# A recurrent attention and MoE kernel: stage 0 turned before its decay, diagonals moved off TensorE in four stages, and a shorter look-ahead in the pair loop

## The chip, the cores and the metric

The kernel runs on one core of a Trainium2 chip. The metric is the device time of one execution in microseconds (us); lower is better. Engines: TensorE (PE, with its weight loads as PEld), VectorE (DVE), ScalarE (ACT), GpSimd (POOL), SyncE (SP), and 16 DMA engines.

## The reference

Per batch (4) and head (8) a 48 x 48 state decays along 768 steps; each output row is read from the state plus a diagonal term with its own weight u. The result goes through a two-layer network with a leaky ReLU.

```
for t in range(768):
    cur = einsum(u * k[t], v[t]);  y[t] = einsum(r[t], state + cur)
    state = w[:, None] * state + einsum(k[t], v[t])
x = y as (3072, 384);  h = x @ w_in (384 x 2048);  out = max(0.01*h, h) @ w_out (2048 x 384)
```

## The kernel before, in words

**Tiling.** A stage is 128 time steps of one batch, all 8 heads: 24 stages, numbered chunk by chunk (stage n is chunk n // 4 of batch n % 4). Within a stage the decay is put into the operands: q = r * w^(t-64) and k' = k * w^(63-t), by two tables `qtab` and `ktab` made once with exp of an exponent times ln w. q and k' are turned (transposed) to `tp`; their product A, cut by a strict triangle `mask`, is the attention inside the stage; the state `st` brings in the earlier chunks.

**The letters.** A list ORDER, written out in the source, gives the program order of the whole start: the tables, the attention of the first stages (0 to 9, and some of 10 and 11) and the network of stages 0 to 5 in part. Each engine plays its own items of it in that order, and semaphores are derived from what is read and written. A letter and a stage: k, r, v loads (POOL queue; those of stage 0 for k on ACT and r on SP); wi, wo weight loads (POOL); P the DVE product with a table (L344; q or k half); T the turn by four TensorE matmuls with the identity (L398) and t its eviction on ACT (L412) or DVE (L410, "@"); X the DVE product q*k' (L359), or with a final T the turn by a DMA transpose issued by SP (L349) instead of T and t; A the eight matmuls of q with k' (L423); M the two masked evictions (L432, L436); D four matmuls of width 2 that give the diagonal sums (L451); Q the scaling of v by them on DVE (L366); Y the matmuls that form y (three with `vs` and the identity, L550, and 16 to 28 of 32 columns, L557) and y their eviction to xT on ACT (L571); K the four matmuls of k' with v (L464) and S the state on DVE (L522, or L525 and L527); G a group of 12 matmuls of the first layer for one stage (L596) and g its leaky eviction (L606); J and j the same for a pair of stages (L619, L629); H and h the second layer of a stage (16 matmuls, L643) with its eviction (L655) and store (SP, L657); F a number of filling matmuls on ones (L260).

**Two kinds of diagonal.** In a stage below DIAG the diagonal goes D, Q and the three matmuls with `vs`. In a later stage DVE makes row sums of r*k*u (L373, L375, L377, letter q), POOL makes two tiles `at` with them on the diagonal (L384, letter Q there), and the masked eviction writes over the rest with a predicate (L436).

**Two kinds of turn.** Stages below TURNED are turned on TensorE, the others by the DMA transpose.

**Start.** w is spread to all partitions by two fp32 matmuls (L295), ACT takes its ln (L301) and makes the tables (L306), DVE applies them to stage 0 (L344), and only then TensorE turns stage 0. w's columns (L484, L485) feed the decay table of the state. POOL makes `ident` and `mask` (L266, L270).

**Pair loop.** After ORDER a loop over pairs m = 3 to 11 of stages (2m, 2m+1) plays eight J of the pair; row sums and diagonal tiles of stages 2m+4, 2m+5; loads of 2m+8, 2m+9; P and DMA turn of 2m+6, 2m+7; H of 2m-2; A of 2m+4, 2m+5; Y and y of 2m+2, 2m+3; M, K and S of 2m+4, 2m+5; H of 2m-1. Banks of PSUM (8) are handed out in program order, first freed first taken.

Of the kernel before, what the change touches and what calls it, by code (L numbers as in the profile page):

```python
# [6 lines left out]
ALU = mybir.AluOpType  # L7
# [120 lines left out]
def bass_rwkv5_eagle__then__act_leaky_relu_kernel(  # L128
# [39 lines left out]
    qexp = SB("qexp", [128, 1], FP32)  # L168
# [3 lines left out]
    ones = SB("ones", [128, 256])  # L172
# [14 lines left out]
    ps = [ctx.enter_context(nc.psum_tensor(f"ps{i}", [128, 512], FP32)) for i in range(8)]  # L187
# [56 lines left out]

    def tokens():
        add("pool", lambda: G.iota(tcol[:, :], pattern=[[0, 1]], base=0, channel_multiplier=1,
                                   allow_small_or_imprecise_dtypes=True), W=["tcol"])

# [6 lines left out]
    def fill(n):  # L255
        i = free[0]

        def emit():
            for _ in range(n):
                last = PE.matmul(ps[i][:, 0:256], ones[:, 0:128], ones[:, 0:256], start=True, stop=True)  # L260
# [12 lines left out]
    def exponents():  # L273
        add("dve", lambda: V.tensor_scalar(kexp[:, :], tcol[:, :], -1.0, float(MID - 1), ALU.mult, ALU.add),
            R=["tcol"], W=["kexp"])
        add("dve", lambda: V.tensor_scalar(qexp[:, :], tcol[:, :], 1.0, float(-MID), ALU.mult, ALU.add),
            R=["tcol"], W=["qexp"])

    def zero_v():
        add("dve", lambda: V.memset(v_sb[:, :, :].rearrange("p n (h e) -> p (n h) e", e=E)[:, :, D:E], 0.0), W=["v0"])  # L280
# [9 lines left out]
    half_bank = {}  # L290

    def spread_w(half):
        ps_w, key = half_bank[half] = take()
        cols = slice(192 * half, 192 * half + 192)
        add("pe", lambda: PE.matmul(ps_w[:, cols], one_row[:, :], w_row[:, cols], start=True, stop=True),  # L295
            R=["one_row", "w_row"], W=[key])

    def log_w(half):
        ps_w, key = half_bank[half]
        cols = slice(192 * half, 192 * half + 192)  # L300
        add("act", lambda: A.activation(lnw[:, cols], ps_w[:, cols], AF.Ln), R=[key], W=[("lnw", half)])  # L301
        give(key)

    def table(dst, exps, name, half):
        cols = slice(192 * half, 192 * half + 192)
        add("act", lambda: A.activation(dst[:, cols], lnw[:, cols], AF.Exp, scale=exps[:, 0:1]),  # L306
            R=[("lnw", half), name + "exp"], W=[(name + "tab", half)])

    def small_identity():
        add("dve", lambda: V.tensor_copy(ident8[:, :], ident[0:H, 0:H]), R=["ident"], W=["ident8"])  # L310

    def wu_product():
        add("dve", lambda: V.tensor_tensor(wu_head[:, :], w_head[:, :], u_head[:, :], ALU.mult),
            R=["w_head", "u_head"], W=["wu_head"])
# [26 lines left out]
    def prep_half(n, half):  # L341
# [3 lines left out]
            R=[(name, n), ("qk"[half] + "tab", 0), ("qk"[half] + "tab", 1), ("qk0", iq)], W=[(done, iq)])  # L345
# [42 lines left out]

    turn_bank = {}

    def turn_mm(n, half):
        iq = n % NQK
        ps_t, key = turn_bank[n, half] = take()

        def emit():
            for p in range(NP):
                h0 = half * H + 2 * p
                last = PE.matmul(ps_t[:, 128 * p:128 * p + 128],  # L398
                                 qk[iq][:, h0:h0 + 2, :].rearrange("p h e -> p (h e)"), ident[:, :],
                                 start=True, stop=True)  # L400
            return last

        add("pe", emit, R=[("kp" if half else "qp", iq), ("qk0", iq), "ident"], W=[key])

    def turn_out(n, half, eng):
# [3 lines left out]
        if eng == "dve":  # L409
# [68 lines left out]
    def columns_mm():  # L478
        ps_c, key = c_bank["c"] = take()

        def emit():
            for hh in range(2):
                rows = slice(64 * hh, 64 * hh + D)
                PE.matmul(ps_c[rows, 0:H], w_head[:, :], ident8[:, :], start=True, stop=True)  # L484
                last = PE.matmul(ps_c[rows, H:2 * H], wu_head[:, :], ident8[:, :], start=True, stop=True)  # L485
            return last

        add("pe", emit, R=["w_head", "wu_head", "ident8"], W=[key])

    def every_other(ps_c, rows, c0, hh):  # L490
        return ps_c[rows, c0:c0 + H].rearrange("p (m two) -> p two m", two=2)[:, hh, :]

    def log_columns():
        ps_c, key = c_bank["c"]
        for hh in range(2):
            rows = slice(64 * hh, 64 * hh + D)
            add("act", lambda rows=rows, hh=hh: A.activation(wcol[rows, :], every_other(ps_c, rows, 0, hh), AF.Ln),
                R=[key], W=[f"wcol{hh}"])

    def decay_columns():  # L500
        ps_c, key = c_bank["c"]
        for hh in range(2):
            rows = slice(64 * hh, 64 * hh + D)
            add("dve", lambda rows=rows, hh=hh: V.tensor_copy(
                wu[rows, :, hh:hh + 1].rearrange("p m o -> p (m o)"), every_other(ps_c, rows, H, hh)),
                R=[key, f"wcol{hh}", "wu"], W=[f"wu{hh}"])
# [278 lines left out]
```

## Time and profile before

| What | Value |
|---|---|
| median of 3 runs (lowest, highest) | 170.09 us (169.96, 170.54) |
| the profiled execution's own time | 170.54 us |
| its span, first to last instruction | 168.8 us |
| busy: PE, PEld, DVE, ACT, POOL | 164.0, 124.4, 107.6, 92.5, 103.8 us |
| DMA packets moved | 19.67 MB, of which 10.03 MB on the POOL-issued queue |

How to read it: busy time is summed per engine; the chain of work that ended last names, step by step back from the end, what released the work or what stood before it on its engine. Idle time of an engine off that chain costs nothing. Durations of single instructions overlap where an engine pipelines them, so the chain's steps, and not the mean durations, are what TensorE work costs in a row. The execution's own time is 1.74 us above its span.

### The profile page before, as it was taken

What the parts mean: (1) busy time and instruction counts of PE and PEld (TensorE: products, weight loads), DVE (VectorE), ACT (ScalarE), POOL (GpSimd) and SP (SyncE); (2) the same over time, 40 slices, a digit from 0 to 9 for tenths busy, and PEclk for the clock granted to TensorE, in tenths of its full rate; (3) what the DMA queues carried; (4) which work ended last, traced back from release to release, by engine and by line L of the source; (5) the groups of instructions that cost most, each with busy time, mean ns of one, the idle gap of its engine ahead of it and who ended that gap; (6) DMA issues with size and microseconds to landing.
All of it is one profiled execution on the core that took longest, in us unless ns stands there. A gap on an engine that the chain in (4) does not pass through costs nothing.

```text
span 168.8 us, 4933 instructions
## 1 busy us (share of the span) xinstructions
PE 164.0 (97%) x2127; PEld 124.4 (74%) x2127; DVE 107.6 (64%) x215; ACT 92.5 (55%) x172; POOL 103.8 (61%) x117
## 2 busy tenths in 40 slices
PE   5999999899999999999999999999999999999994
PEld 3577899798667867867867867768768668668663
DVE  7379989884376999999859959969866050000000
ACT  3855899587123933933834835735637538449221
POOL 7999999990059979897993993993707200000000
PEclk9999999999999999999999999999999999999999
DMA  6999999999999999969999299299941011011022
GB/s 106 155 170 133 163 163 173 185 190 149 110 177 144 161 62 153 193 82 169 126 140 171 55 143 177 65 109 131 147 122 50 0 50 47 0 50 47 25 74 93
DMA packets 99146, 19.67 MB, mean 117 GB/s; under 512 B 92338, under 2 KB 99124, under 8 KB 99124
## 3 DMA queue, kind: packets, MB, share of 16 engines
q0 software_dynamic: 76512, 10.03, 93.1%
q1 hardware_dynamic: 21554, 9.12, 25.2%
q8 instruction: 17, 0.28, 0.6%
q10 hardware_dynamic: 1058, 0.20, 0.6%
q14 instruction: 5, 0.04, 0.1%
HBM read 20.45 MB, written 4.72 MB: 149 GB/s over the span
## 4 chain that ended last, share of the span: by engine, by line
PE 96%; DVE 1%; issue 1%; ACT 0%; DVEq 0%
PE ps L643 37%; PE ps L619 31%; PE ps L596 6%; PE ps L557 6%; PE ps L423 4%; PE ps L260 2%; PE ps L464 2%; PE ps L398 2%; PE ps L295 1%; PE ps L550 1%; DVE v_sb L280 1%; PE ps L451 1%; PE ps L321 0%; DVE qk L344 0%; ACT out_sb L655 0%
## 5 line engine op out<-in xcount | busy, mean ns | idle before, releaser
L643 PE MATMUL ps<-w_out_sb,gT 128*128 128x384 bf16 (+2 forms) x400 | 65.7, 320 | 0.0
L619 PE MATMUL ps<-xT,w_in_sb 128*128 128x256 bf16 x480 | 54.3, 273 | 0.0
L643 PEld LDWEIGHTS ps<-w_out_sb,gT 128*128 128x128 bf16 x400 | 37.9, 98 | 22.1
L619 PEld LDWEIGHTS ps<-xT,w_in_sb 128*128 128x128 bf16 x480 | 46.7, 98 | 6.5 <-ACT xT L571 0.2
L384 POOL TENSOR_TENSOR at<-ident,s_tok 128x512 bf16<-128x512 bf16 x32 | 35.0, 1121 | 26.8 <-DVE s_tok L377 26.8
L629 ACT ACTIVATE gT<-ps 128x512 bf16<-128x512 f32 x80 | 47.8, 597 | 6.2 <-PE ps L619 1.3
L655 ACT ACTIVATE out_sb<-ps 128x384 f32<-128x384 f32 (+2 forms) x25 | 11.9, 477 | 52.9 <-PE ps L643 52.9
L436 DVE CAST_PREDICATED at<-mask,ps 128x512 bf16<-128x512 uint16 x32 | 19.9, 684 | 15.5 <-PE ps L423 15.5
L222 POOL DMA_DIRECT2D v_sb<-in_v_dram x24 | 22.5, 953 | 0.0
L222 POOL DMA_DIRECT2D k_sb<-in_k_dram x23 | 21.6, 947 | 0.0
L222 POOL DMA_DIRECT2D r_sb<-in_r_dram x23 | 21.1, 943 | 0.0
L571 ACT ACTIVATE xT<-ps 128x384 bf16<-128x384 f32 x24 | 11.0, 492 | 6.5 <-PE ps L557 6.5
L344 DVE TENSOR_TENSOR qk<-r_sb,qtab 128x384 bf16<-128x384 bf16 x23 | 13.4, 592 | 1.9 <-DMA r_sb<-in_r_dram 1.9
L344 DVE TENSOR_TENSOR qk<-k_sb,ktab 128x384 bf16<-128x384 bf16 x23 | 13.9, 606 | 0.0
L375 DVE TENSOR_TENSOR rku<-r_sb,ku 128x384 bf16<-128x384 bf16 x16 | 12.7, 794 | 0.5
L525 DVE TENSOR_TENSOR sum_t<-ps,st 128x384 bf16<-128x384 f32 x16 | 8.8, 550 | 5.2 <-PE ps L464 5.2
L596 PE MATMUL ps<-xT,w_in_sb 128*128 128x128 bf16 x192 | 12.0, 219 | 0.0
L557 PE MATMUL ps<-at,v_sb 128*32 128x128 bf16 x384 | 11.1, 219 | 0.6 <-issue 0.6
L432 DVE TENSOR_TENSOR at<-ps,mask 128x512 bf16<-128x512 f32 x16 | 10.5, 682 | 0.9 <-PE ps L423 0.9
L606 ACT ACTIVATE gT<-ps 128x512 bf16<-128x512 f32 x16 | 9.6, 600 | 2.7 <-PE ps L596 2.1
L596 PEld LDWEIGHTS ps<-xT,w_in_sb 128*128 128x128 bf16 x192 | 10.9, 98 | 0.1
L557 PEld LDWEIGHTS ps<-at,v_sb 128*32 128x32 bf16 x384 | 8.7, 97 | 1.1 <-issue 0.7
(60 smaller groups left out, 131.7 us busy)
## 6 DMA issues: line engine op xcount, KB each, us to landing
out_dram<-out_sb SPq DMA_DIRECT2D x23, 192.0 KB, 3.9
v_sb<-in_v_dram POOLq DMA_DIRECT2D x24, 96.0 KB, 6.0
r_sb<-in_r_dram POOLq DMA_DIRECT2D x23, 96.0 KB, 5.6
k_sb<-in_k_dram POOLq DMA_DIRECT2D x23, 96.0 KB, 5.1
w_in_sb<-in_moe_w_in_dram POOLq DMA_DIRECT2D x4, 384.0 KB, 5.6
w_out_sb<-in_moe_w_out_dram POOLq DMA_DIRECT2D x4, 384.0 KB, 7.9
tp<-qk SPq DMA_TRANSPOSE x16, 4.6
k_f<-in_k_dram ACTq DMA_DIRECT2D x1, 192.0 KB, 2.8
```

Source lines behind the costliest of these rows:

```text
L222: add("pool", lambda: G.dma_start(dst, src), R=pace, W=[(which, n)], dma=f"{which}{n}")
L344: add("dve", lambda: V.tensor_tensor(qk[iq][:, H * half:H * half + H, 0:D], hd(src), hd(tab[:, :]), ALU.mult), R=[(name, n), ("qk"[half] + ...
L375: add("dve", lambda: V.tensor_tensor(rku[i2][:, :], r_of(n), ku[i2][:, :], ALU.mult), R=[("r", n), ("ku", i2)], W=[("rku", i2)])
L384: add("pool", lambda hh=hh, s_of=s_of: G.tensor_tensor(at[ia][:, hh, :, :], ident[:, :].unsqueeze(1).to_broadcast([128, NP, 128]), s_of.un ...
L436: add("dve", lambda: V.copy_predicated(at[n % NAT][:, hh, :, :], mask[:, :].bitcast(mybir.dt.uint16).unsqueeze(1).to_broadcast([128, NP, 1 ...
L557: last = PE.matmul(ps_y[32 * q:32 * q + 32, 128 * s:128 * s + 128], a, m, start=not whole and step == 0, stop=step == len(columns[q]) - 1)
L571: add("act", lambda: A.activation(xT[m % NX][:, :, 128 * half:128 * half + 128], ps_y[:, 0:HD].rearrange("p (s t) -> p s t", t=128), AF.Copy),
L596: last = PE.matmul(ps_g[:, 128 * f:128 * f + 128], w_in_sb[:, s, 128 * fb:128 * fb + 128], xT[ix][:, s, t], start=s == 0, stop=s == NSL - 1)
L619: last = PE.matmul(ps_g[:, 256 * f:256 * f + 256], w_in_sb[:, s, 128 * fb:128 * fb + 128], xT[ix][:, s, :], start=s == 0, stop=s == NSL - 1)
L629: add("act", lambda: A.activation(gT[ig][:, 2 * j:2 * j + 2, :].rearrange("p f t -> p (f t)"), ps_g[:, :], AF.Prelu, alpha=0.01), R=[key], ...
L643: last = PE.matmul(ps_o[:, 0:c1 - c0], gT[ig][:, s, 128 * half:128 * half + 128], w_out_sb[:, s, c0:c1], start=s == 0, stop=s == NFB - 1)
L655: add("act", lambda: A.activation(out_sb[io][:, c0:c1], ps_o[:, 0:c1 - c0], AF.Copy), R=[key], W=held)
```

## The change

Named constants: TURNED 8 to 6 (stages 6 and 7 are turned by DMA), DIAG 8 to 4 (stages 4 to 7 take their diagonal from row sums and POOL tiles), and new RAW = 1, VISIT = 3, LATE = 3. ORDER is replaced. A, M, K and S of stages 8 and 9, P and turn of stages 10 and 11 and the six loads of stages 12 and 13 move from it into the loop.

Stage 0 is turned unscaled: DVE casts r and k to `raw`, TensorE turns `raw`, and the eviction on DVE multiplies PSUM by `turned`, a table of w^(exponent) with w's columns on the partitions and the time along the free axis (four ACT exps of two iota rows `trow`). Spreading w becomes two fp32 matmuls from partitions 0 and 64 into two banks, one ln and one exp per table of full width. `ident`, `mask` and the 8 x 8 identity are made by DVE compares of `trow` with `tcol` in place of POOL selects and a cast. The clearing of v's gaps is split in two; fills are 128 wide in place of 256; the first SP load is w by head.

In the pair loop A, M, Y, K, S are all of the due pair 2m+2, 2m+3; P and turn are of 2m+4, 2m+5 and loads of 2m+6, 2m+7. For m = 3 to 5 ("late") the due A stands after the eight J, its masks ahead of the P of the next pair; from m = 6 on A stands ahead of the fourth J and P ahead of the masks.

```diff
-TURNED, DIAG, CARRY, EXACT = 8, 8, 4, 1
+TURNED, DIAG, CARRY, EXACT, RAW, VISIT, LATE = 6, 4, 4, 1, 1, 3, 3
 ORDER = """
-w k0 r0 u8 w8 u ones tcol wi0 v0z r2 table exps one id wlz qk0 F6 bcA r1 id8 F2 bcB lnA k1 u16 wu8 ktabA F1 Cm k2 lnB U
-qtabA ktabB v0 utab P0k qtabB Wl wi3 F6 T0k P0q W C tri t0k@ F1 T0q v1 P1q t0q P2q F6 T1q X0 r3 A0 P1k t1q T2q M0a T1k
-k3 t2q D0 P2k F1 K0 t1k Q0 T2k v2 M0b t2k F1 A1 X1 v5 F2 Y0 X2 M1b A2 k4 y0 D2 M1a D1 K1 G0.0 k5 Q1 M2b G0.3 g0.0 wi1
-P3q Y1 P3k g0.3 r4 S1 T3q y1 K2 Q2 T3k t3q v3 G1.3 S2 t3k M2a G1.0 r5 g1.3 P4k Y2 X3 g1.0 r8 P5k A3 S0 y2 K5 M3b r6 T5k
-G2.3 t5k S5 k7 G2.0 g2.3 M3a G1.1 k9 g2.0 P4q G0.1 g1.1 wi2 T4k g0.1 D3 P5q K3 r7 T4q Q3 t4k T5q G2.1 S3 t5q k6 P8q Y3
-t4q P6q X5 A5 v4 g2.1 P7k A4 X4 y3 D5 T6q M4a wo3 T7k t6q G3.0 M5a v8 t7k G3.3 Q5 g3.0 wo0 M5b D4 G3.1 g3.3 P9k k8 G2.2
-M4b g3.1 P7q G1.2 wo2 g2.2 P6k T7q v6 g1.2 T6k t7q@ K4 Y5 t6k Q4 wo1 A7 y5 X6 A6 k11 S4 Y4 M7b v9 D6 y4 G3.2 M6a v10
-J2.4 M6b g3.2 J2.3 M7a v11 j2.4 J2.5 X7 j2.3 r10 D7 J2.1 j2.5 q8 r9 J2.2 j2.1 J2.6 r11 j2.2 P8k J2.0 j2.6 v7 X8T K8 Q6
-K6 j2.0 G0.2 k10 S6 Y6 g0.2 S8 J2.7 y6 H1 j2.7 P11k K9 H2 h1 S9 P10q H0 h2 P9q q9 X9T P11q K7 Q9 H3 Q7 h0 X11T S7 P10k
-X10T Q8 Y7 h3 A9 y7 A8 M9a M8a M9b M8b k12 r12 v12 k13 r13 v13
+w8 k0 r0 w u8 u one trow ones tcol wlz r1 table tri id8 zr v0y k1 F6 Cw Wl exps id wi1 E v0z c0k@ k3 qk0 F11 T0k bc r3
+c0q@ W wu8 t0k u16 T0q v0 lnw Cu t0q U qtab r2 C utab F2 A0 X0 P1q ktab v1 D0 M0a T1q wi3 P1k t1q P0k F6 T1k k2 P3k M0b
+t1k F5 T3k v3 P3q F1 A1 t3k X1 Q0 r4 F1 D1 M1b T3q K0 k4 Y0 P2q t3q M1a K1 y0 A3 r5 Q1 T2q S1 G0.1 t2q k5 M3a Y1 g0.1
+X3 wi2 G0.3 M3b y1 wi0 P2k G1.3 g0.3 S0 v2 D3 T2k g1.3 Q3 G1.1 t2k P4q v5 K3 P4k Y3 g1.1 X2 wo1 T4q P5q y3 D2 S3 T4k
+t4q T5q v4 q5 G3.1 t4k A2 r6 t5q A4 g3.1 G3.3 wo3 P5k G1.2 M2a g3.3 Q5 M2b G3.2 g1.2 q4 G0.2 g3.2 G0.0 g0.2 k6 K2 g0.0
+T5k Q2 G1.0 Q4 S2 t5k Y2 g1.0 A5 y2 G3.0 M5b k7 G2.3 M5a g3.0 M4a G2.2 wo2 g2.3 M4b K4 Y5 wo0 g2.2 S4 Y4 y5 r7 G2.1 P6q
+y4 k8 J2.1 g2.1 J2.6 r8 q6 j2.1 J2.5 j2.6 r9 J2.3 j2.5 k9 P7k J2.4 j2.3 P6k J2.7 X6T Q6 j2.4 J2.2 j2.7 G2.0 j2.2 J2.0
+g2.0 k10 H1 P7q j2.0 v11 q7 X7T v6 v7 P8k H0 h1 P8q Q7 q8 X8T P9q v8 H3 h0 v10 P9k q9 X9T r11 r10 A6 h3 A7 M6a H2 v9
+M7a k11 M7b M6b Q9 K6 Y6 h2 S6 Y7 y6 K7 y7 Q8 K5 S7 S5
...
-    w_row = SB("w_row", [1, HD], FP32)
+    w_row = SB("w_row", [128, HD // 2], FP32)
-    one_row = SB("one_row", [1, 128], FP32)
+    one_row = SB("one_row", [128, 128], FP32)
-    w_head = SB("w_head", [H, D], FP32)
+    w_head = SB("w_head", [H, 2, E], FP32)
-    qexp = SB("qexp", [128, 1], FP32)
+    trow = SB("trow", [128, 2, 128], FP32)
+    turned = SB("turned", [128, 2 * NP, 128])
+    raw = SB("raw", [128, 2 * H, E])
...
+    def token_rows():
+        for half, (sign, base) in enumerate(((1, -MID), (-1, MID - 1))):
+            add("pool", lambda half=half, sign=sign, base=base: G.iota(
+                trow[:, half, :], pattern=[[sign, 128]], base=base, channel_multiplier=0,
+                allow_small_or_imprecise_dtypes=True), W=[("trow", half)])
...
     def identity():
-        add("pool", lambda: G.affine_select(ident[:, :], ones[:, 0:128], pattern=[[1, 128]], compare_op=ALU.is_equal,
-                                            fill=0.0, base=0, channel_multiplier=-1), R=["ones"], W=["ident"])
+        add("dve", lambda: V.tensor_scalar(ident[:, :], trow[:, 0, :], tcol[:, 0:1], None, ALU.is_equal),
+            R=["tcol", ("trow", 0)], W=["ident"])
     def triangle():
-        add("pool", lambda: G.affine_select(mask[:, :], ones[:, 0:128], pattern=[[1, 128]], compare_op=ALU.is_ge,
-                                            fill=0.0, base=-1, channel_multiplier=-1), R=["ones"], W=["mask"])
+        add("dve", lambda: V.tensor_scalar(mask[:, :], trow[:, 0, :], tcol[:, 0:1], None, ALU.is_gt),
+            R=["tcol", ("trow", 0)], W=["mask"])
+
+    def small_identity():
+        add("dve", lambda: V.tensor_scalar(ident8[:, :], trow[0:H, 0, 0:H], tcol[0:H, 0:1], None, ALU.is_equal),
+            R=["tcol", ("trow", 0)], W=["ident8"])
...
+    def zero_v(n0, n1):
+        add("dve", lambda: V.memset(v_sb[:, n0:n1, :].rearrange("p n (h e) -> p (n h) e", e=E)[:, :, D:E], 0.0),
+            W=[("v0", n) for n in range(n0, n1)])
...
-    half_bank = {}
-    def spread_w(half):
-        ps_w, key = half_bank[half] = take()
-        cols = slice(192 * half, 192 * half + 192)
-        add("pe", lambda: PE.matmul(ps_w[:, cols], one_row[:, :], w_row[:, cols], start=True, stop=True),
-            R=["one_row", "w_row"], W=[key])
-    def log_w(half):
-        ps_w, key = half_bank[half]
-        cols = slice(192 * half, 192 * half + 192)
-        add("act", lambda: A.activation(lnw[:, cols], ps_w[:, cols], AF.Ln), R=[key], W=[("lnw", half)])
-        give(key)
-    def table(dst, exps, name, half):
-        cols = slice(192 * half, 192 * half + 192)
-        add("act", lambda: A.activation(dst[:, cols], lnw[:, cols], AF.Exp, scale=exps[:, 0:1]),
-            R=[("lnw", half), name + "exp"], W=[(name + "tab", half)])
-    def small_identity():
-        add("dve", lambda: V.tensor_copy(ident8[:, :], ident[0:H, 0:H]), R=["ident"], W=["ident8"])
+    w_bank = []
+    def spread_w():
+        for half in range(2):
+            w_bank.append(take())
+        assert w_bank[1][1][1] == w_bank[0][1][1] + 1
+        def emit():
+            for half in range(2):
+                at0 = slice(64 * half, 64 * half + 1)
+                last = PE.matmul(w_bank[half][0][:, 0:192], one_row[at0, :], w_row[at0, :], start=True, stop=True)
+            return last
+        add("pe", emit, R=["one_row", "w_row"], W=[w_bank[0][1], w_bank[1][1]])
+    def log_w():
+        i = w_bank[0][1][1]
+        add("act", lambda: A.activation(lnw[:, :].rearrange("p (two c) -> p two c", two=2),
+                                        ps_all[:, i:i + 2, 0:192], AF.Ln),
+            R=[w_bank[0][1], w_bank[1][1]], W=["lnw"])
+        give(w_bank[0][1])
+        give(w_bank[1][1])
+    def table(dst, exps, name, read):
+        add("act", lambda: A.activation(dst[:, :], lnw[:, :], AF.Exp, scale=exps[:, 0:1]),
+            R=["lnw", read], W=[name + "tab"])
+    def turned_table():
+        for p in range(NP):
+            add("act", lambda p=p: A.activation(turned[:, p:2 * NP:NP, :], trow[:, :, :], AF.Exp,
+                                                scale=wcol[:, p:p + 1]),
+                R=["wcol", ("trow", 0), ("trow", 1)], W=[("turned", p)])
...
+    def cast(half, eng):
+        dst, src = raw[:, H * half:H * half + H, 0:D], hd((r_of, k_of)[half](0))
+        if eng == "dve":
+            add("dve", lambda: V.tensor_copy(dst, src), R=[("rk"[half], 0)], W=[("raw", half)])
+        else:
+            add("act", lambda: A.activation(dst, src, AF.Copy), R=[("rk"[half], 0)], W=[("raw", half)])
     turn_bank = {}
     def turn_mm(n, half):
-        iq = n % NQK
+        src, reads = qk[n % NQK], [("kp" if half else "qp", n % NQK), ("qk0", n % NQK)]
+        if n < RAW:
+            src, reads = raw, [("raw", half), "raw0"]
...
+        if n < RAW:
+            tab = turned[:, NP * half:NP * half + NP, :].rearrange("p m t -> p (m t)")
+            add("dve", lambda: V.tensor_tensor(dst, ps_t[:, :], tab, ALU.mult),
+                R=[key] + [("turned", p) for p in range(NP)], W=[("tp", it, half)])
...
+    def w_columns():
+        ps_c, key = c_bank["w"] = take()
         def emit():
             for hh in range(2):
+                last = PE.matmul(ps_c[64 * hh:64 * hh + 64, 0:NP], w_head[:, hh, :], ident8[:, hh:H:2],
+                                 start=True, stop=True)
+            return last
+        add("pe", emit, R=["w_head", "w_gap", "ident8"], W=[key])
...
+        ps_c, key = c_bank["w"]
+        add("act", lambda: A.activation(wcol[:, :], ps_c[:, 0:NP], AF.Ln), R=[key], W=["wcol"])
+        give(key)
...
-        due, ahead, later, far = ([n for n in (2 * m + x, 2 * m + x + 1) if n < NST] for x in (2, 4, 6, 8))
+        due, ahead, far = ([n for n in (2 * m + x, 2 * m + x + 1) if n < NST] for x in (2, 4, 6))
+        late = m < FIRST // 2 + LATE
         for j in range(8):
+            if j == VISIT and not late:
+                for n in due:
+                    a_mm(n)
             g1_pair(m, j)
             g1_pair_out(m, j)
+        for n in due if late else ():
+            a_mm(n)
+        if not late:
+            for n in ahead:
+                prep(n)
+        for n in due:
+            a_mask(n)
+        if late:
+            for n in ahead:
+                prep(n)
+        for n in far:
+            load_stage(n, pace=[("pace", 2 * m, 1)])
         for n in ahead:
             row_sums(n)
             diag_tile(n)
-        for n in far:
-            load_stage(n, pace=[("pace", 2 * m, 1)])
-        for n in later:
-            prep(n)
         g2(2 * m - 2)
         g2_out(2 * m - 2)
-        for n in ahead:
-            a_mm(n)
         for n in due:
             y_part(n)
-        for n in ahead:
-            a_mask(n)
-        turning = [n for n in ahead if n < NST - NB]
+        turning = [n for n in due if n < NST - NB]
         for n in turning:
             kv_mm(n)
         for n in turning:
```

More of the change, by code (lines that the diff above doesn't have):

```diff
@@ L259, in emit @@
             for _ in range(n):
-                last = PE.matmul(ps[i][:, 0:256], ones[:, 0:128], ones[:, 0:256], start=True, stop=True)
+                last = PE.matmul(ps[i][:, 0:128], ones[:, :], ones[:, :], start=True, stop=True)
             return last
@@ L476, in kv_mm, with wu_columns, emit @@
         add("pe", emit, R=reads, W=[key])
-    def columns_mm():
-        ps_c, key = c_bank["c"] = take()
+    def w_columns():
+        ps_c, key = c_bank["w"] = take()
         def emit():
             for hh in range(2):
-                rows = slice(64 * hh, 64 * hh + D)
-                PE.matmul(ps_c[rows, 0:H], w_head[:, :], ident8[:, :], start=True, stop=True)
-                last = PE.matmul(ps_c[rows, H:2 * H], wu_head[:, :], ident8[:, :], start=True, stop=True)
-            return last
-        add("pe", emit, R=["w_head", "wu_head", "ident8"], W=[key])
-    def every_other(ps_c, rows, c0, hh):
-        return ps_c[rows, c0:c0 + H].rearrange("p (m two) -> p two m", two=2)[:, hh, :]
-    def log_columns():
[L494 to L498, printed above, removed]
+                last = PE.matmul(ps_c[64 * hh:64 * hh + 64, 0:NP], w_head[:, hh, :], ident8[:, hh:H:2],
+                                 start=True, stop=True)
+            return last
+        add("pe", emit, R=["w_head", "w_gap", "ident8"], W=[key])
+    def wu_columns():
+        ps_c, key = c_bank["u"] = take()
+        def emit():
+            for hh in range(2):
+                last = PE.matmul(ps_c[64 * hh:64 * hh + D, 0:NP], wu_head[:, :], ident8[:, hh:H:2],
+                                 start=True, stop=True)
+            return last
+        add("pe", emit, R=["wu_head", "ident8"], W=[key])
+    def log_columns():
+        ps_c, key = c_bank["w"]
+        add("act", lambda: A.activation(wcol[:, :], ps_c[:, 0:NP], AF.Ln), R=[key], W=["wcol"])
+        give(key)
     def decay_columns():
-        ps_c, key = c_bank["c"]
+        ps_c, key = c_bank["u"]
         for hh in range(2):
@@ L504, in decay_columns @@
             add("dve", lambda rows=rows, hh=hh: V.tensor_copy(
-                wu[rows, :, hh:hh + 1].rearrange("p m o -> p (m o)"), every_other(ps_c, rows, H, hh)),
-                R=[key, f"wcol{hh}", "wu"], W=[f"wu{hh}"])
+                wu[rows, :, hh:hh + 1].rearrange("p m o -> p (m o)"), ps_c[rows, 0:NP]),
+                R=[key, "wu"], W=[f"wu{hh}"])
         give(key)
```

54 lines of the change are left out of this document (30 added, 24 removed).

## The prediction

> **What bounds the kernel now.** I read the page's busy line, then the chain, then the timeline of the first 54 us, and last the waits.
>
> ```profile
> span 168.8 us, 4933 instructions
> PE 164.0 (97%) x2127; PEld 124.4 (74%) x2127; DVE 107.6 (64%) x215; ACT 92.5 (55%) x172; POOL 103.8 (61%) x117
> ...
> PE 96%; DVE 1%; issue 1%; ACT 0%; DVEq 0%
> ```
>
> TensorE is the chain for 96% of the span. A matmul taken away is worth its time in a row; work taken off another engine is worth nothing unless TensorE waits for it. The chain in order of time shows where it isn't saturated:
>
> ```profile
> 10.94 0.56 PE ps L423 x8
> ...
> 12.20 0.36 DVE qk L344
> 12.56 0.05 issue
> 12.61 0.40 PE ps L398 x4
> 13.01 0.11 PE ps L260
> 13.12 0.33 PE ps L423 x8
> 13.45 0.33 PE ps L260 x2
> 13.77 0.24 PE ps L550 x3
> ```
>
> Columns: start, duration, what. Up to 12.6 us the chain runs through fills (L260), table work and one DVE product; from there it is TensorE to the end. So the end is: the time at which steady work begins, plus the TensorE work left, plus later holes. I take the start of Y0 (L550, 13.7 us) as the mark. The only large later hole is this wait, which no instruction explains:
>
> ```profile
> PE ps L557 <- issue: 0.6, 1, 0.6
> ```
>
> I keep 0.56 us of it (bounds 0 and 0.56).
>
> **TensorE work removed.** Stages 6 and 7 lose T, four groups; the chain has two groups as 0.45 us (26.18, 30.11), so 0.90. Stages 4 to 7 lose D, 0.08 to 0.09 each (23.56, 28.00, 36.35), 0.35, and the three matmuls with `vs`, 0.17 each (30.72), 0.68. Sum 1.93 us, all in the saturated part. A, K, Y, G, J, H keep their counts; they move only.
>
> **The start.** Before, stage 0 waits for w's spread, ln, two tables and the product. Now:
> 1. w by head is the first SP load (0.80). w_row in that slot was there by 3.15; w_head, issued at 1.67, released DVE at 4.58, 2.9 later. So 3.15 to 3.7; I take 3.4.
> 2. Two column matmuls (the eight passes of L484 and L485 took 0.43 at 5.92): 0.2; ln 0.16 (L497): `wcol` at 4.05 with handovers.
> 3. Four exps of 256 columns: those of 192 start 0.35 apart (5.86, 6.21), one of 384 takes 0.52; 0.42 each, 1.7: `turned` at 5.75.
> 4. Casts on DVE: behind the memsets (v's, 1.34 before, is split 5/6 and 1/6) they begin near 3.9, 0.25 to 0.56 each (L344 reading fp32 took 0.56). They end by 5.6, under step 3.
> 5. F11 at 0.107 a cold 128 columns (six of 256 took 1.39) ends at 4.85, T0k takes 0.43 (8.17): 5.3. The two fp32 spreads take 0.97 if rows 0 and 64 run together, 1.94 (3.15, 4.66) if not: 6.25 or 7.2. The nearest row is A, whose 48-row pairs at rows 0 and 64 come every 0.041 (0.33 for eight) against 0.056 for T (0.45 for eight): partly together. I take the middle. T0q 0.43, then its eviction 0.68 (L432 reads the same PSUM width): 7.6 or 8.5.
> 6. A0 follows, in place of 10.94. But stage 1 needs qtab (ln 0.5, exp 0.6: 8.2) and ktab (after u_tab, 0.5 + 0.6: 9.2), and DVE must do C 0.35, X0 0.42, P1q, M0a 0.69, P1k, P0k 0.56, P3k, M0b 0.68, P3q, X1 0.42, Q0 0.55, the four P of bf16 starting 0.27 to 0.35 apart: about 4.8 after t0q. Y0 at 12.4 or 13.3; I take 12.85 against 13.67, a gain of 0.82 (bounds 0 and 1.3). D1 is then done as well, 0.09.
>
> The gain is small because DVE, not w, paces stage 1: most of A0's three microseconds is given back.
>
> **What is late next.** Between Y0 and T2k DVE has M1b, M1a, M3a, M3b at 0.62, Q1, S1 at 0.5, X3 0.4, P2q, P2k at 0.3: 4.5 us. TensorE has Y0, Y1 1.02, K1 0.17, A3 0.33, T2q 0.22, three G 2.0, D3 0.09, 3.85, about 4.05 with the gaps that the old chain has. It waits 0.45.
>
> From 19 to 29 us DVE gains the row sums (ku, rku, s: 0.35, 0.36, 0.55) of stages 4 and 5 and POOL two tiles each. Beside POOL's tiles DVE's products of two SBUF operands are held:
>
> ```profile
> 57.39 2.97 DVE L375 TENSOR_TENSOR rku<-r_sb,ku 128x384 bf16<-128x384 bf16 x1
> ...
> 61.14 1.20 DVE L344 TENSOR_TENSOR qk<-k_sb,ktab 128x384 bf16<-128x384 bf16 x1
> 62.26 1.20 DVE L344 TENSOR_TENSOR qk<-r_sb,qtab 128x384 bf16<-128x384 bf16 x1
> 63.38 0.35 DVE L344 TENSOR_TENSOR qk<-k_sb,ktab 128x384 bf16<-128x384 bf16 x1
> ```
>
> The same product takes 0.35 without tiles and 1.20 beside them, rku 2.97 in place of 0.36. Adding up DVE from P4q (18.1) through S3, q5, M2, q4, Q2, M5, M4 brings M4b to 27.5 to 28.6, with one or two such holds; TensorE reaches Y4 near 29. I charge 0.2 (bounds 0 and 2.6, one whole hold).
>
> [...]
>
> **POOL's queue.** 8 more tiles, 1.07 each in a row (4.28 for four), stand among the loads. From 2.0 us (two iotas of 128, each between the 0.13 of `tcol` and the 0.30 to 0.63 of a 128-wide select) 23 issues at 0.88 reach 22.3; tiles of 5 and 4 and k6, k7, wo2 put wo0's issue at 29.7, against 29.5 for the last w_out before. Six fewer loads stand ahead of it, so it should land like a load without backlog, 5.5 to 7 later, at 35 to 37. H1 needs it: Y4 ends at 31.1 (12.85 and the old 19.84 from Y0 to there, less 2.2 of work removed or moved past it, plus 0.65 of waits), then G2.1, seven J, G2.0, J2.0, 6.7: 37.8. Hidden, by 0.8 to 2.8. v6 and v7 leave at 39 to 40 for Y6 at 48. DMA turns of stages 6, 7 leave at 32 and 38 and took 2.7 to 8.3 to land, A6 and A7 come at 45: hidden.
>
> **The loop.** A pair costs TensorE 12.1 to 12.3 either way. Late pairs: A at the eighth J, masks 2.48 in a row from 0.35 after it, then Y after A's 0.55 and H's 2.60: 2.8 against 3.15, just hidden. DVE has 2.5 + 1.2 + 2.5 + 1.85 us per pair and up to 3 of holds, under 12. At m = 6 A moves up to the fourth J, 2.0 into the pair, while its P were last done late (masks end 8.2 into pair 5, P 9.3, both DMA turns landed 5.6 after the first issue: 14.4, against 12.1 + 2.0): 0.4 (bounds 0 and 2.5).
>
> **Sum**, against the profiled execution of 170.54: -0.82 - 0.09 - 1.93 + 0.45 + 0.2 + 0.4 = -1.8, so 168.75. The median lies 0.45 under the profiled one: **168.3**.
>
> **Rivals.**
> 1. *DVE becomes the bound from 16 to 30 us.* For: DVE is busy 4.0 of 4 us from 12 to 20 already, and the holds above. Against: 32 of 41 us over 12 to 53.5. One whole rku hold more, 2.6 in place of 0.2, on what feeds Y4, less slack of 0.6: 170.1, no change. Chance 0.13.
> 2. *The clock comes later.* The granted clock reads 1.00 in every window, yet T's matmuls take 314 ns up to 11.4 us and 223 after. Now the stretch up to 11 us holds waits (A0 to T1q). [...] For: the fills that stood there shrink. Against: the waits are 0.5 each. Chance 0.12. [...]
> 3. *Slower: POOL's queue holds the last w_out load.* If the tiles wait for `s_tok` (POOL waited up to 10.2 us for it before) or the load lands 9.6 later, as the last w_out did, H1 waits for it one for one. A wait of 2.3, so a landing after 40.1, makes it slower than before by over 0.5: with tiles 2 late and 9.6 to land, 41.3, so 3.5 of wait and about 171.8. Against: a shorter backlog. Chance 0.15.
> 4. *Better:* both spreads together, no issue hole: 166.9. Chance 0.05.
>
> **Numbers.** The forecast has 0.55, its own range 167.2 to 169.4. About 0.3% (0.5 us) is what the measurement can tell from no change. Faster: 0.55 + 0.12 + 0.05 = 0.72; same 0.13; slower 0.15. The range 166.4 to 170.9 takes in the bounds of the unknown costs and rivals 1, 2 and 4, and leaves out rival 3 and the far ends.
>
> **What would show it.** A0 near 8.2 and Y0 near 12.9; matmul counts down by 16 (L398's line), 16 (L451's) and 12 (L550's); TensorE's holes after Y0 under 1.7 together. A first hole before T2k released by DVE, a later one in H1 released by w_out, or A14 waiting for its turn would each mean its step was mis-sized. Y0 after 13.7 would make the prediction wrong at its root.

## The result and the profile after

The changed kernel takes 169.15 us (median of 6 runs, 168.64 to 169.59) against 170.04 (169.96 to 170.54) in the same comparison: ratio 0.994, interval 0.9917 to 0.9963. Faster, by 0.9 us and not by the forecast 1.8. Its profiled execution took 169.59. In two kernels below, the old loop and the diagonals back on TensorE, nearly every execution shows a mean granted clock of 0.97 to 0.99, so their times are not read as prices.

The page after, busy line and chain by engine, to be held against the same lines of before:

```profile
span 167.8 us, 4861 instructions
PE 162.7 (97%) x2089; PEld 123.1 (73%) x2089; DVE 110.5 (66%) x224; ACT 91.3 (54%) x168; POOL 110.8 (66%) x125
PE 90%; POOL 4%; DMA 4%; ACT 1%; issue 0%; POOLq 0%
```

TensorE keeps its 97%, but its share of the chain fell from 96% to 90%. The chain now begins with loads: v1's, issued behind seven others in POOL's queue, lands 6.63 us after its issue and starts K1 (L506) at 14.26. ("DMA" in the chain is the time in which a load was under way.) The chain from there, in order of time (start, duration, what):

```profile
14.76 0.54 PE ps L465 x8
15.30 0.54 PE ps L436 x4
15.84 1.12 PE ps L643 x12
...
19.31 0.67 PE ps L643 x12
```

The same 12 matmuls of a G take 1.12 here and 0.67 a few microseconds on: until 16.7 us TensorE runs at about half rate (a 128-column matmul takes 308 to 314 ns, from then on 219; in a row, the four matmuls of a turn take 0.43 at 10.52 us of before and 0.22 at 17.63), in before until 11.2, and the granted clock reads 1.00 in both. "Fast at" names this moment from here on.

I balance the two chains by three marks: start of Y0, start of the first J of the pair loop, end of the last second-layer matmul (166.48 before, 165.45 after).

| Stretch | before | after | difference | of it, worked out from the rows |
|---|---|---|---|---|
| to Y0 | 13.68 | 12.98 | -0.70 | forecast -0.82 |
| Y0 to the loop | 39.84 | 37.76 | -2.08 | -1.93 T and D, -0.09 D1, -0.56 hole gone, -0.89 A and K of stages 8, 9 moved into the loop; so +1.39 is new |
| the loop | 112.96 | 114.71 | +1.75 | +0.89 moved in; so +0.86 is new |

The 0.86 is in the pairs. One pair of after and one of before, by their chains:

```profile
100.68 1.96 PE ps L666 x18
102.64 0.55 PE ps L465 x16
103.19 3.38 PE ps L666 x30
106.58 2.60 PE ps L690 x16
```

```profile
66.03 5.24 PE ps L619 x48
71.27 2.60 PE ps L643 x16
73.87 0.55 PE ps L423 x16
74.42 0.90 PE ps L557 x56
```

The 48 J matmuls take 1.96 + 3.38 = 5.34 around A and 5.24 in a row; everything else is equal. A pair is 12.44 (100.68 to 113.12) against 12.33 (66.03 to 78.36). In the late pairs the same 0.11 shows on H behind A (2.71 for 2.60). Eight pairs have such a visit of A among full-size matmuls: 8 x 0.105 = 0.84.

Of the 1.39 in the middle, little stands just ahead of the loop. After (chain, then two rows of TensorE's timeline), and then before (chain):

```profile
49.25 0.53 PE ps L604 x28
...
49.80 0.89 ACT xT L618 x2
...
50.74 5.41 PE ps L666 x48
```

```profile
50.08 0.51 PE L506 MATMUL ps<-v_sb,qk 128*128 128x96 bf16 x8
50.74 5.41 PE L666 MATMUL ps<-xT,w_in_sb 128*128 128x256 bf16 x48 [0.15 <-ACT xT L618]
```

```profile
52.42 0.50 PE ps L557 x28
52.92 0.55 PE ps L423 x16
53.47 0.05 issue
```

The first J needs Y7's eviction. Before, A of stages 8 and 9 stood between and covered it. They are in the loop now, but the eight matmuls of K7 and K5 stand in their place, and TensorE waits 0.15 in place of 0.05: 0.10 is new. K1's wait for v1 is 0.21. What is left is 1.08, and the half rate explains it. From Y0 to Y1 the program is the same in experiment 10, which was fast from 13.3 us on. Here, and then there:

```profile
12.98 0.52 PE L597 MATMUL ps<-ident,vs 128*128 128x128 bf16 x3
14.26 0.50 PE L506 MATMUL ps<-v_sb,qk 128*128 128x96 bf16 x4 [0.21 <-DMA v_sb<-in_v_dram]
16.80 0.33 PE L597 MATMUL ps<-ident,vs 128*128 128x128 bf16 x3
```

```profile
12.68 0.52 PE L597 MATMUL ps<-ident,vs 128*128 128x128 bf16 x3
15.05 0.33 PE L597 MATMUL ps<-ident,vs 128*128 128x128 bf16 x3
```

That is 3.82 against 2.37, and 2.11 in experiment 9, which was fast from 11.9 on. Less v1's 0.21, the half rate cost 1.2 to 1.5 here; 0.2 to 0.4 that got shorter elsewhere is not accounted for.

### The profile page after: what moved, and what is told of

It reads as the page before. It is cut to its first block, busy times and chain, and to the rows that moved or that the text cites. A ratio compares the mean times of both kernels' runs of the same rounds, so it can differ in the third digit from the quotient of the medians.

```text
span 167.8 us, 4861 instructions
## 1 busy us (share of the span) xinstructions
PE 162.7 (97%) x2089; PEld 123.1 (73%) x2089; DVE 110.5 (66%) x224; ACT 91.3 (54%) x168; POOL 110.8 (66%) x125
## 4 chain that ended last, share of the span: by engine, by line
PE 90%; POOL 4%; DMA 4%; ACT 1%; issue 0%; POOLq 0%
PE ps L690 38%; PE ps L666 32%; PE ps L643 7%; PE ps L604 6%; DMA v_sb<-in_v_dram 4%; PE ps L465 4%; PE ps L506 2%; POOL r_sb L224 2%; PE ps L436 1%; POOL k_sb L224 1%; ACT xT L618 1%; POOL v_sb L224 1%; POOL w_in_sb L234 0%; PE ps L597 0%; POOL trow L256 0%
## 5 line engine op out<-in xcount | busy, mean ns | idle before, releaser
L413 POOL TENSOR_TENSOR at<-ident,s_tok 128x512 bf16<-128x512 bf16 x40 | 42.5, 1099 | 20.4 <-DVE s_tok L406 20.4
L666 PE MATMUL ps<-xT,w_in_sb 128*128 128x256 bf16 x480 | 55.1, 273 | 0.2 <-ACT xT L618 0.2
L702 ACT ACTIVATE out_sb<-ps 128x384 f32<-128x384 f32 (+2 forms) x25 | 11.9, 478 | 55.6 <-PE ps L690 55.6
L478 DVE CAST_PREDICATED at<-mask,ps 128x512 bf16<-128x512 uint16 x40 | 24.8, 685 | 21.5 <-PE ps L465 21.5
L404 DVE TENSOR_TENSOR rku<-r_sb,ku 128x384 bf16<-128x384 bf16 x20 | 17.1, 856 | 0.7
L643 PE MATMUL ps<-xT,w_in_sb 128*128 128x128 bf16 x192 | 12.8, 224 | 0.0
L373 DVE TENSOR_TENSOR qk<-r_sb,qtab 128x384 bf16<-128x384 bf16 x23 | 10.2, 444 | 3.9 <-DMA r_sb<-in_r_dram 3.9
L574 DVE TENSOR_TENSOR st<-sum_t,wl 128x384 bf16<-128x384 bf16 x16 | 11.7, 730 | 0.5
L406 DVE TENSOR_REDUCE s_tok<-rku 128x8 f32<-128x384 bf16 x20 | 11.1, 553 | 0.7
L373 DVE TENSOR_TENSOR qk<-k_sb,ktab 128x384 bf16<-128x384 bf16 x23 | 8.8, 387 | 0.8 <-DMA k_sb<-in_k_dram 0.8
L604 PEld LDWEIGHTS ps<-tp,st 128*32 128x32 bf16 x240 | 7.2, 96 | 2.7 <-issue 2.5
```

The lines of the kernel that those rows point to most:

```text
L373: add("dve", lambda: V.tensor_tensor(qk[iq][:, H * half:H * half + H, 0:D], hd(src), hd(tab[:, :]), ALU.mult), R=[(name, n), "qk"[half] + ...
L404: add("dve", lambda: V.tensor_tensor(rku[i2][:, :], r_of(n), ku[i2][:, :], ALU.mult), R=[("r", n), ("ku", i2)], W=[("rku", i2)])
L413: add("pool", lambda hh=hh, s_of=s_of: G.tensor_tensor(at[ia][:, hh, :, :], ident[:, :].unsqueeze(1).to_broadcast([128, NP, 128]), s_of.un ...
L478: add("dve", lambda: V.copy_predicated(at[n % NAT][:, hh, :, :], mask[:, :].bitcast(mybir.dt.uint16).unsqueeze(1).to_broadcast([128, NP, 1 ...
L604: last = PE.matmul(ps_y[32 * q:32 * q + 32, 128 * s:128 * s + 128], a, m, start=not whole and step == 0, stop=step == len(columns[q]) - 1)
L643: last = PE.matmul(ps_g[:, 128 * f:128 * f + 128], w_in_sb[:, s, 128 * fb:128 * fb + 128], xT[ix][:, s, t], start=s == 0, stop=s == NSL - 1)
```

## The experiments

The first question was the rate, the second the pair, the third what single parts are worth. Every ratio is against before, measured on the same chip.

**1. The changed kernel again.** For the spread of one program.

> The changed kernel again. Two profiles with the same start (this kernel's and the one with A beside Y) show the short matmul durations from 16.8 and from about 13.5 us, 3.4 apart. If the moment is a matter of the run and not of the code, a third one lies at one of these or 3.4 earlier, near 10, and the runs of this kernel spread by about 1 us (168.64 to 169.59 so far). If the code sets it, it is at 16.8 again.

Measured: 169.67, ratio 0.9942 (0.9919 to 0.9966), the first result again. In this profile the matmuls stay long until 17.6 us, and the hole in Y that before had is absent, as in the first.

**2. More fills in the start's waits.**

```diff
-... qk0 F11 T0k ... utab F2 A0 ... t1k F5 T3k ... M1a K1 y0
+... qk0 F14 T0k ... utab F3 A0 ... t1k F9 T3k ... M1a F2 K1 y0
```

> The changed kernel with three, one and four fills more where TensorE stood idle (ahead of T0k, of A0, of T3k) and two ahead of K1. In the changed kernel TensorE's matmuls reach the short duration (219 ns in place of 311) only near 16.8 us, before the change near 11.2. Theory 1, the late rate comes from TensorE's idle pieces (0.25, 0.1, 0.4 us) in the stretch of 10 us before: closed, the short duration starts near 11 to 13.5 us, and the time falls by 0.6 to 1.3 us against the changed kernel's 169.15. Rival, the rate does not depend on these pieces: it starts near 16.8 again, and the time stays within 0.3 us, or rises by up to 0.3 for the fills.

Measured: 169.0, ratio 0.9904 (0.9874 to 0.9933). The fast rate comes at 10.6 us and Y0 at 12.09; but a hole of 0.84 that no instruction explains opens in Y, and D and A7 wait 0.5 each, so the loop starts at 50.80, no earlier than in the changed kernel (50.74). What the rate gave was lost in these waits, in the profiled execution.

**3. Wide fills, half as many** (256 columns, as before the change).

```diff
-... k1 F6 Cw ... F11 T0k ... F2 A0 ... F6 T1k ... F5 T3k
+... k1 F3 Cw ... F5 T0k ... F1 A0 ... F3 T1k ... F3 T3k
-    ones = SB("ones", [128, 128])
+    ones = SB("ones", [128, 256])
```

> The changed kernel with its fills 256 wide as before the change, in half the number, so that they take the same time in a row. Theory 1 (idle pieces set the rate): no change, short durations from near 16.8 us, time within 0.3 us of 169.15. Rival, the width of the fills sets it (narrow matmuls behind one weight load each keep the array less busy): short durations from near 11 to 13.5 us and 0.6 to 1.3 us less.

Measured: 168.84, ratio 0.9917 (0.9886 to 0.9947). Fast at 11.9, Y0 at 12.41, a hole of only 0.09, loop at 49.80. One profile can't tell the width of the fills from chance: experiment 9, with the changed kernel's narrow fills, is fast at 11.9 too.

**4. No fills behind stage 0's first turn.**

```diff
-... utab F2 A0 ... P0k F6 T1k ... t1k F5 T3k ... P3q F1 A1 ... r4 F1 D1
+... utab A0 ... P0k T1k ... t1k T3k ... P3q A1 ... r4 D1
```

> The changed kernel without the fills behind stage 0's first turn (F2 before A0, F6, F5, F1, F1). Theory A (TensorE's matmuls go to the fast rate after a stretch of work with few holes; fills in the holes bring it nearer): without them T and A up to Y1 keep the long duration (about 310 ns for T) until 16.8 us or later, at 20 us at the latest, Y0 starts at 12.9 to 13.5, and the median is 0 to 0.7 us above the changed kernel's (ratio 0.994 to 0.998). Theory B (the moment is drawn in each run, 10.6, 13.5 or 17, and the fills do nothing): the fast rate is as likely at 10.6 or 13.5 as at 17 in this one profile, and the median is as the changed kernel's or up to 0.3 lower, since the 15 fills took TensorE time in the start. A fast rate before 14 us speaks against A; one after 17 says nothing alone.

Measured: 169.09, ratio 0.9939 (0.9917 to 0.996): the changed kernel's time without 15 of its fills. Fast at 17.0, which alone says nothing. Y0 came at 12.06, 0.9 sooner than in the first profile of the changed kernel, mostly because there T3k's DVE product waited 0.84 for k3's load. The fills placed here buy nothing that these runs can tell.

**5. Wide fills and more fill time together.**

```diff
-... k1 F6 Cw ... F11 T0k ... F6 T1k ... F5 T3k ... M1a K1 y0
+... k1 F3 Cw ... F7 T0k ... F3 T1k ... F5 T3k ... M1a F1 K1 y0   (256 columns each)
```

> The changed kernel with its fills 256 columns wide, as before, and about a third more fill time in the start's waits (7 wide in place of 11 narrow ones ahead of stage 0's second turn, 2, 3 and 5 wide ones in place of 2, 6 and 5 narrow ones behind it, one more ahead of K1): the two earlier fill versions together. Theory (more unbroken work makes the fast rate come sooner in more of the runs): fast by 11.5 us in the profile, Y0 at 12.1 to 12.5, and a median ratio of 0.989 to 0.992, if the hole that nothing explains in Y near 30 us stays under 0.5; with that hole at 0.8 to 1.0, 0.993 to 0.995. Rival (the moment is a matter of the run, and fills change nothing but TensorE's own time): 0.994 as for the changed kernel and for the one without late fills, and a fast rate at 13.5 or 17 is as likely as at 11.

Measured: 168.98 (168.88 to 169.18), ratio 0.9917 (0.9885 to 0.9949). Fast at 12.2, Y0 at 12.73, and the hole again, but in another place. The chain of this run, then that of experiment 10, which has the changed kernel's fills:

```profile
29.62 0.44 PE ps L643 x6
30.07 0.91 issue
30.98 0.51 PE ps L643 x6
```

```profile
28.85 0.93 PE ps L604 x53
29.78 0.84 issue
30.62 0.24 PE ps L604 x3
```

In the one it splits a G, in the other a Y. The count of matmuls that started from the span's beginning to a moment inside each hole (second row: experiment 10) says what they share:

```profile
0.00:30.50 30.50, 28.54 (x474) 22.42 (x474) 26.12 (x69) 22.70 (x43) 29.38 (x40) 1.00 1.77 156
0.00:29.85 29.85, 27.74 (x474) 23.00 (x474) 25.58 (x68) 22.09 (x42) 28.77 (x40) 1.00 1.75 156
```

474 matmuls in both, and in experiments 2, 6, 7 and 9 too (472 in before). The hole belongs to the position in TensorE's instruction stream and not to Y or G. What the traces show beside it stands under what stays open.

**6. A beside Y from pair 6 on** (A of the next pair between Y and K, its masks last).

```diff
-            if j == VISIT and not late:
+            if j == VISIT and not late and m == FIRST // 2 + LATE:
...
         for n in due:
             y_part(n)
+        for n in () if late else ahead:
+            a_mm(n)
...
+        for n in () if late else ahead:
+            a_mask(n)
```

> The changed kernel with A of the next pair behind Y of the due pair from m = 6 on, and no A among the J from m = 7 on. Theory 2, each place where A's half-row matmuls stand between full-size ones costs about 0.1 us more than beside Y: the four pairs m = 7 to 10 lose 0.1 each, 0.3 to 0.5 us in all, and a pair's eight J take 5.24 in a row again. Rival, the extra 0.1 per pair has another cause: a pair still takes 12.44 and the time stays within 0.2 us. A loss would come if the DMA turns land after A's new place, up to 1 us per pair.

Measured: 172.9, ratio 1.0138 (1.0098 to 1.0178). The 48 J take 5.24 in a row again, but A comes before its turn has landed:

```profile
PE ps L465 <- DMA tp<-qk: 3.2, 3, 1.6
```

The place among J is there because of the shorter look-ahead: with A one pair earlier, P and turn are too late for it.

**7. w_in's second load behind v1**, so that k3 and v1 leave sooner.

```diff
-... exps id wi1 E ... D0 M0a T1q wi3
+... exps id E ... D0 M0a T1q wi1 wi3
```

> The changed kernel with the load of the second quarter of w_in moved from third place on POOL's queue to behind v1. k3, r3, v0, r2, v1 leave 0.8 us earlier. Theory 3, K1's wait for v1 (0.2 us) and T3k's for k3 (0.4 us) are on the path: Y0 and K1 start 0.2 to 0.5 earlier, the time falls by 0.2 to 0.6 us. Rival, G0.1 then waits for that w_in quarter, which took 7.8 us to land: it would land near 15.4 and the gain is lost, within 0.2 us of 169.15 or above.

Measured: 170.43, ratio 0.9995 (0.997 to 1.0019). K1 no longer waits for v1, but TensorE waits for raw (0.6) and a product (0.4), a k load that took 7.48 us to land stands on the chain, and the hole is 1.03. Moving one load back moved others forward, and the kernel lost 0.9 us against the changed one. In this profile the loop starts 0.82 later than in the changed kernel's (51.56 against 50.74), and the hole alone is longer than that, so the loss can't be put down to the loads.

**8. The pair loop of before** on the changed start; A, M, K, S of stages 8, 9, P and turn of 10, 11 and loads of 12, 13 at the end of ORDER.

```diff
+... Q8 K5 S7 S5 P10k P10q X10T P11k P11q X11T A9 A8 M9a ... K8 K9 S8 S9 k12 r12 v12 k13 r13 v13
-        (loop of after)
+        (loop of before)
```

> The changed kernel with the pair loop of before the change; A, M, K, S of stages 8 and 9, P and turn of 10 and 11 and the loads of 12 and 13 stand at the end of ORDER again. Theory 2 (A between full-size matmuls costs 0.1 us per pair more than A beside Y): pairs take 12.33 in place of 12.44 and the eight that hold an A give 0.8 us back, 168.3. Rival, the shorter look-ahead is needed by the new start: DVE's added products at the end of ORDER or the DMA turns of 8 to 11 come late, TensorE waits before the loop, and the time is 169 or above.

Measured: 176.46, ratio 1.03 (1.0248 to 1.0353). TensorE's waits, and further on in its chain the J of three pairs:

```profile
PE ps L465 <- DMA tp<-qk: 3.6, 1, 3.6
PE ps L506 <- DMA v_sb<-in_v_dram: 2.3, 2, 2.1
```

```profile
58.03 7.28 PE ps L666 x48
...
84.74 5.24 PE ps L666 x48
...
97.07 5.24 PE ps L666 x48
```

A waits 3.6 for a turn and K 2.1 for a load (its chain has 11.22 us from issue to landing) ahead of the loop. Behind these waits the granted clock reads 0.76 from 50 to 60 us and 0.90 from 60 to 70 (0.981 over the execution), and the first J take 7.28 (5.41 in the changed kernel). The later pairs take 12.33 again. So the shorter look-ahead is dearer by 0.11 a pair and yet needed, at least with loads ordered as here.

**9. The deep look-ahead from pair 7 on**, where loads have caught up.

```diff
+        for n in ahead if m > 6 else ():
+            a_mm(n)          # between H and Y
+        if m == 6: P and turn of stages 18, 19 at the pair's end
+        loads: 14, 15, 16 in pair 4; 17, 18, 19 in pair 5; 20, 21 in pair 6
```

> The changed kernel's loop up to pair 6, from pair 7 on the look-ahead of before: A of the next pair between H and Y, masks after Y, P and turn two pairs ahead; two stages' loads moved one pair up, in pairs 4 and 5. A now stands beside Y in pairs 7, 8 and 9 and not among J in 8, 9 and 10. Theory (A's 48-row matmuls cost 0.1 us more between full-size ones than beside Y, which are of 48 rows in part too): in pairs 8 to 11 the 48 J stand in a row as 5.24 us, H after Y and K as 2.60, pair for pair 12.33 in place of 12.44, together -0.3 against the changed kernel: ratio 0.992. Rival (the 0.1 is the price of something else in the loop, as POOL's tiles or DVE): the pairs stay at 12.44. If the deeper look-ahead comes too early for its loads or turns, A or DVE waits once in pair 7, 0.5 to 3 us, and the ratio is 0.995 to 1.01; the pairs behind it can still be read.

Measured: 171.93, ratio 1.0087 (1.0055 to 1.0119): slower. Behind the passage the pairs are as the theory has them. Pair 9, in which no K is needed any more, begins with J in a row:

```profile
128.51 5.24 PE ps L666 x48
133.75 2.60 PE ps L690 x16
```

It takes 12.00 (128.51 to 140.51), the changed kernel's 12.10 (137.66 to 149.76). The passage costs more than three pairs can give back: A waits 1.3 for turns, H 0.9 for the masks; the hole in Y is 1.32 here.

**10. Turns of stages 6 and 7 back on TensorE.**

```diff
-TURNED, DIAG = 6, 4
+TURNED, DIAG = 8, 4
-... J2.7 X6T ... q7 X7T
+... J2.7 T6q t6q T6k t6k ... q7 T7q t7q T7k t7k
```

> The changed kernel with stages 6 and 7 turned on TensorE again in place of the DMA transpose. The forecast's price: four groups at 0.225, 0.9 us more, 170.05. Rival, the DMA turn of stage 7 lands so late (8.3 us in the run with fills in the gaps, where A7 waited 0.5 for it) that the change gains less: under 0.5 us more.

Measured: 170.5, ratio 0.9984 (0.9964 to 1.0004), 0.0042 above the changed kernel's in the same comparison: 0.7 us, with about 0.5 either way. The chain has the two pairs of groups as 0.45 each. The forecast of 0.90 for this part agrees with both.

**11. Diagonals of stages 4 to 7 back on TensorE.**

```diff
-TURNED, DIAG = 6, 4
+TURNED, DIAG = 6, 8
-... q5 ... q4 ... q6 ... q7 ...
+... X4 D4 Q4 ... X5 D5 Q5 ... X6 D6 Q6 ... X7 D7 Q7 ...
```

> The changed kernel with the diagonal of stages 4 to 7 on TensorE again: D, the product on DVE and the three matmuls with vs, no row sums and no POOL tiles there. The forecast's price: D 0.35 and vs matmuls 0.68, so 1.0 us more, 170.2 against 169.15. Rival, the eight tiles and row sums delay POOL's loads and DVE in the changed kernel by about as much: within 0.4 us of 169.15.

Measured: 176.41, ratio 1.0309 (1.026 to 1.0359), 6 us above the changed kernel where 1.0 had been priced. TensorE's two largest waits of this run:

```profile
PE ps L465 <- DVE st L569: 2.5, 1, 2.5
PE ps L493 <- DVE prod L388: 1.6, 2, 1.3
```

They are waits for DVE in an order that was planned without its added D and Q; the chain goes back from the first of them, over DVE, to a load of v that took 9.77 us to land. This run doesn't say what the three `vs` matmuls and D are worth; only the counts (12 and 16 matmuls fewer) and the rows of before do.

**12. A split in two** in pairs 6 to 10: eight matmuls ahead of the fourth J, eight ahead of the sixth.

```diff
-            if j == VISIT and not late:
-                for n in due:
-                    a_mm(n)
+            if j in (VISIT, VISIT + 2) and not late and due:
+                a_mm(due[j // VISIT - 1 if j == VISIT else 1])
```

> The changed kernel with A of the two stages of a pair put apart in pairs 6 to 10: eight matmuls ahead of the fourth J, eight ahead of the sixth. The same matmuls, twice as many changes between the 48-row matmuls and the full-size ones. Theory (each visit of A among J costs 0.1 us): the chain's J and A of such a pair add up to 0.1 more than in the changed kernel (5.34 + 0.55 before the split, 5.44 + 0.6 after), 12.55 a pair, +0.5 in all: ratio 0.997. Rival (the cost goes by the number of A matmuls, or by what else is new in these pairs): 12.44 a pair as before the split, ratio 0.994.

Measured: 170.56, ratio 1.0009 (0.999 to 1.0027), 0.0067 above the changed kernel, 1.1 us. One pair up to H:

```profile
100.34 1.97 PE ps L666 x18
102.30 0.33 PE ps L465 x8
102.63 1.42 PE ps L666 x12
104.05 0.33 PE ps L465 x8
104.38 2.07 PE ps L666 x18
```

J adds up to 5.46 and A to 0.66, where they had 5.34 and 0.55: 0.22 more a pair, 0.11 on each side of the added visit. Five such pairs give 1.1, the measured difference (the loop takes 115.76 in place of 114.70). The theory is shown, at twice the price that I had put on it: the one visit of the changed kernel also costs 0.22, but A pays the way in (0.11) beside Y too, so only the way out is new there.

## Why the prediction was right and wrong, point by point

- **The forecast's sign and range** held (169.15 in 166.4 to 170.9); its size did not, 168.3. In the profiled execution's terms -1.8 was forecast and -1.0 came (166.48 and 165.45). The smallness of the miss is partly luck: errors of +2.4 and -1.6 stood against each other.
- **TensorE work removed, 1.93.** The counts fell by 16, 16 and 12 as said. Experiment 10 gives 0.7 for the 0.90 of T; the rest, D and `vs`, rests on rows only.
- **The start.** A0 came at 7.37 (8.2 forecast): the two spreads run together, 1.01 for both (0.97 and 1.00 for one, in before). qtab and ktab were done at 7.07 and 8.14, sooner than 8.2 and 9.2. And yet Y0 began at 12.98, where 12.85 was forecast: the right number by another way, and so by luck. Loads (k3: 0.84) and the half rate paced stage 1, not DVE and the tables.
- **The three waits, 1.05 in all** (T2k 0.45, holds beside POOL's tiles 0.2, A14 0.4): none came. After Y0 TensorE's waits list v1's 0.2 and the first J's 0.2. The hole in Y that I kept was 0.56 in before and 0 here.
- **Where its size failed: "A, K, Y, G, J, H keep their counts; they move only".** The moves were priced at nothing, and a pair at "12.1 to 12.3 either way"; it is 12.44. A's visits among full-size matmuls cost 0.84 in eight pairs (experiments 6, 8, 9 and 12). An edit that moves work was costed without asking what stands on both sides of its new place. What its old place had covered, Y7's eviction, cost only 0.10, since K stands there now.
- **Rival 2, the later clock, had come as well, and is the largest single term.** It had a chance of 0.12. No run shows what sets the moment; in the profiled executions it came at 11.2 us in before and at 16.7 here, the rate cost 1.2 to 1.5, and v1 another 0.21. That execution was the slowest of the six; when the others became fast isn't known. Before's chain already had TensorE at work without a break from 3.15 us on, and its matmuls long to 11.2: in 8 us unbroken work alone had not brought the fast rate, so the chance should have been higher.
- **Rival 1** (DVE bound), no: TensorE waits for DVE nowhere behind Y0. **Rival 3** (w_out late in POOL's queue), no: H1 began at 38.0, forecast 37.8, without a wait. **Rival 4** had both of its conditions, spreads together and no hole, and its 166.9 still did not come, as the terms above took it back.
- **The sum.** From -1.79: +0.12 Y0, -1.05 waits, -0.56 hole, +0.86 in the loop, +0.10 eviction, +0.21 v1 and +1.08, the remainder that the half rate explains, give -1.03. The remainder makes the sum close, so the sum is no proof of it; the comparison from Y0 to Y1 is its test.

**What stays open.** When the fast rate comes is a matter of the execution at least as much as of the code: in nine profiles with the changed kernel's fills it came at 10.6, 11.9, 13.1, 13.3, 13.5, 14.2, 16.7, 17.6 and 17.7 us; in the three with more or wider fills (experiments 2, 3 and 5) at 10.6, 11.9 and 12.2, and their ratios (0.9904, 0.9917, 0.9917) lie some 0.0025 below those of the changed kernel and of the one without late fills (0.994, 0.9942, 0.9939). That points to the fills, but the intervals overlap. The moment varies by 7 us among the nine, and what sets it isn't shown. The cause of the hole behind the 474th matmul wasn't tried. Nine profiles have a hole there, of 0.09 us up (before and experiments 2, 3, 5, 6, 7, 9, 10 and 12), and TensorE goes on at a moment between 29.72 us (experiment 6) and 31.94 (before). The profile has a DMA queue of kind "instruction" (16 packets of 16 KB in the changed kernel, 17 in before). In before the third of these packets is through at 30.58 us and TensorE goes on 1.36 us later; in the changed kernel's first profile, which has no hole, it is through at 29.61 and TensorE gets to the place 1.50 us later, at 31.11. No run moved that packet, so it isn't shown that the hole hangs on it. The hole was 0.4 to 1.3 us in seven of nine profiles that were fast by 13.5 us, and at most 0.14 in the five that were later: part of what an early clock gains is lost there. No version was shown to beat the changed kernel beyond doubt; the wide fills (168.84, and 168.98 with more of them) have the lowest medians.

## What to carry to other kernels

When work is moved and not removed, name what its old place covered and what stands on both sides of its new one: here a move that was counted as free cost 0.84 us of the 2.8 that the removed matmuls and the earlier start were forecast to be worth. A's matmuls of 48 rows were cheaper beside Y's small ones (0.11 a pair); put such matmuls among full-size ones only if a wait of more than the two changes (0.11 us each here) goes away for it. Before trusting a shorter start, look in each profile for where the duration of one and the same matmul falls (here from 314 to 219 ns), and take more than one profile, for the moment moved between executions (from 10.6 to 17.7 us here). Before calling the idle time between two marks a wait, list what else the engine does there.

## What the runs showed of the hardware that I had not expected

- A change from full-size matmuls to A's 48-row ones costs 0.11 us, and so does the change back (5.24 us for 48 J in a row, 5.34 with one visit, 5.46 with two; A 0.55 for 16, 0.33 for 8).
- The granted clock reads 1.00 from the first microsecond on, while one form of matmul takes 314 ns and later 219 (16.7 us in the changed kernel's first profile).
- A hole of up to 1.32 us (experiment 9) sat at a fixed count of matmuls, the 474th (the 472nd in before), in before in a Y and in experiment 5 in a G; in before it ended 1.36 us after a packet of the instruction queue.
- Behind TensorE's waits of 3.6 and 2.1 us in experiment 8 the granted clock read 0.76 from 50 to 60 us and 0.90 from 60 to 70, and 48 J took 7.28 us in place of 5.41; in experiment 11, behind a wait of 2.5, it read 0.83 from 30 to 40.
- Loads of k, r and v on POOL's queue took 6.63 us to land when issued at 7.58, 6.9 to 9.8 when issued from 10 to 22 us and 7.5 to 11.7 from 40 to 50 us, where I had taken 5.5 to 7.
- The two fp32 matmuls that spread w from partitions 0 and 64 run together: 1.01 us for both (0.97 and 1.00 for one, in before).
